# Attention and a routed two-layer expert network on one core: spacers that bring x and W1 to one residue modulo 512 bytes

## The chip, the core and the metric

The kernel runs on one core of a Trainium2 chip. The metric is device time in microseconds. Of the core's engines this text names PE (TensorE; its weight loads stand in a row of their own, PEld), DVE (VectorE), ACT (ScalarE), POOL (GpSimd) and SP (SyncE, here a DMA queue).

## What is computed

Shapes: 8 batches, 8 heads, 576 positions, head size 64; 8 experts, model width 512, hidden width 1024; all float32.

```python
kv = np.einsum('bhsd,bhse->bhde', k, v)
out = np.einsum('bhsd,bhde->bhse', q, kv)
rms = np.sqrt(np.mean(out * out, axis=-1, keepdims=True) + 1e-06)
x = (out / rms * g_norm)                      # transposed to (B, S, H * D)
...
logits = np.einsum('bsd,de->bse', x, w_gate)
local_gate = 1.0 / (1.0 + np.exp(-np.einsum('bsd,de->bse', x, w_local).squeeze(-1)))
for b in range(B):
    prev_e = -1
    for s in range(S):
        fresh_e = int(np.argmax(logits[b, s]))
        e = fresh_e if s == 0 or local_gate[b, s] < 0.5 else (prev_e if prev_e >= 0 else fresh_e)
        prev_e = e
        ...                                   # p: softmax of logits[b, s]
        h = np.maximum(x[b, s] @ w1[e], 0.0)
        out[b, s] = p[e] * (h @ w2[e])
```

Each of the 4608 tokens goes through the one expert that the routing names.

## The kernel before

**Up to about 167 us** the kernel computes the linear attention, writes its rows to DRAM, works out the routing, and does four 128-token blocks of expert 0: two together (`first_wide`, line 1079, from `xh`, `xl` that lie in an attention buffer) and two singly (`block`, line 1114, whose activations are the tiles `th`, `tl`).

**From there to the end** runs the loop of line 1442 over seven ranks, the other experts in order of their load. Each rank has 768 to 512 tokens, in two parts. The tokens' rows are gathered from DRAM (POOL), scaled, transposed and split (ACT, DVE) into a high and a low part: tiles `xh`, `xl` for the first part of a rank, `yh`, `yl` for the second, each of 4 depths by 384 columns (`xtiles(xp, HM, ...)`, lines 1412, 1459 and 1487). The matrices come by DMA into `wst` and are split into high and low parts in the same way (`wsplit`, line 257).

A float32-accurate product is made of three matmuls in the fp32r type, high by high, high by low, low by high (`split_mm`, line 1001; lines 1005, 1010, 1011). A part of a rank goes through

- a first product (`first_wide`): W1 is loaded as weights, 128 columns at a time, and x or y streams past it with 384, 352, 320 or 256 columns; 8 column blocks by 4 depths by 3 terms are 96 matmuls, accumulated in `ph`; ACT and DVE make `hh`, `hl` of it;
- a second product for each 128 tokens (`products`, line 1020): `hh`, `hl` as weights, W2 streams with 512 columns; 8 by 3 are 24 matmuls into `py` (a last block of 64 tokens goes through line 1055).

The order on PE, DVE, ACT and POOL is written by hand: it is the order of the code, with hooks (`then`, `hooks`, `tick`) that put scales, transposes, splits and gathers between the matmuls. Buffers come from stacked pools, so a tile's address is the sum of what lies before it. `pad` (line 157) puts a tile that nobody uses into a pool; its third argument counts 4-byte elements, 16 without it, and a pad of a name already seen is left out.

**Where the tiles lie.** The pool `xp` holds x, the six gather buffers `xr`, then y and the transposes' `xT`. Right behind it the pool `b` holds the W1 slots 4 to 7 and the W2 slots 4 and 5. The W1 slots 0 to 3 are in the pool `s`. `wsplit` gives a rank one group of four W1 slots and the next rank the other: rank 1 has slots 4 to 7, rank 2 has 0 to 3, and so on. The names in the trace leave the layer out: `w_4h` beside `ph` is slot 4 of W1, beside `py` slot 4 of W2. Inside all these tiles the steps between depths and column blocks are multiples of 512 bytes, so each operand of a matmul has the residue of its tile.

Of the kernel before, what the change touches and what calls it, by code (L numbers as in the profile page):

```python
# [22 lines left out]
def kernel(  # L23
# [124 lines left out]
    wpools = {}  # L148

    def wpool(nm, side="right"):  # L150
        wpools[nm] = wstack.enter_context(
            tc.tile_pool(name="w" + nm, bufs=1, side=side, reuse_waits="tile"))
        return wpools[nm]
# [3 lines left out]
    def pad(pool, nm, n=16):  # L157
        if nm not in padded:
            padded.add(nm)
            pool.tile([P, n], F32, name=nm)  # L160
# [85 lines left out]

    def wtile(pool, nm):
        if nm in ("w2_0h", "w2_4h"):
            pad(wpools[pool], "pad" + pool, 112 if pool == "s" else 48)
        t = wpools[pool].tile([P, 2 * DM], F32R, name=nm)  # L250
        if nm == "w2_0l":
            pad(wpools[pool], "past" + pool, 32)
        if nm == "w2_2l":
            pad(wpools[pool], "pad" + pool)
        return t

    def wsplit(e, i, two=False):
        t = staged.pop((e, i))

        if i < NW1:  # L260
            slot = (e * NW1 + i) % (2 * NW1)
            nm, pool = f"w1_{slot}", "s" if slot < NW1 else "b"
        else:
            slot = (e * NW2 + i - NW1) % (NW2 + 2)
            nm, pool = f"w2_{slot}", "scc"[slot] if slot < 3 else "d" if slot < NW2 else "b"
        hi, lo = (wtile(pool, nm + x) for x in "hl")
        low_ = split_w(hi, lo, t, i, e > 1)
        wt[e, i] = (hi, lo)

        def low(engine=nc.vector):  # L270
            i = low_(engine)
            if to_load:
                wload(*to_load.pop(0))
            return i

        if two:
            return low
        low()
# [800 lines left out]
    def first_wide(w, hh, hl, xh, xl, n=2 * P, then=(), each=None, late=0):  # L1079

        st = 2 if n <= 2 * P else 1
        then = list(then)

        def pairs(f, d0, d1):
            return [(w1s(w, d, f * P, P), (xh[:, d, 0:n], xl[:, d, 0:n])) for d in range(d0, d1)]

        if late:
            phs = [ps_h.tile([P, 1, n], F32, name="ph", tag="bank") for _ in range(late)]
            for f in range(late):
                split_mm(phs[f][:, 0], pairs(f, 0, ND - 1), last=False)  # L1090
                for what in then[f:f + 1]:
                    if what:
                        what()
            for f in range(late):
                split_mm(phs[f][:, 0], pairs(f, ND - 1, ND), first=False)
                relu_split(hh[:, f:f + 1, 0:n], hl[:, f:f + 1, 0:n], phs[f], n)
        for f in range(late, NF, st):
            ph = ps_h.tile([P, st, n], F32, name="ph", tag="bank")
            for x in range(st):
                split_mm(ph[:, x], pairs(f + x, 0, ND))  # L1100

            nl = n - n % P if n % P == D else n
            relu_split(hh[:, f:f + st, 0:n], hl[:, f:f + st, 0:nl], ph, nl)
            if nl < n:
                nc.vector.scalar_tensor_tensor(
                    hh[:, f:f + st, n:n + D], ph[:, :, nl:], 0.0,
                    hh[:, f:f + st, nl:n].bitcast(F32), op0=ALU.max, op1=ALU.subtract)
            if each:
                each()
            for what in then[f:f + st]:  # L1110
                if what:
                    what()
# [38 lines left out]
    def htiles(pool, n=2 * P):  # L1151
        return tuple(pool.tile([P, NF, n], F32R, name="h" + x) for x in "hl")

    def xtiles(pool, n, nm):
        return tuple(pool.tile([P, ND, n], F32R, name=nm + x, bufs=2 if nm == "t" else 1)
                     for x in "hl")
# [101 lines left out]
    xp = wpool("xp", "left")  # L1258
# [5 lines left out]
    def read(c, most):  # L1264
        return nc.values_load(cnt[0:1, c:c + 1], min_val=0, max_val=most)  # L1265
# [135 lines left out]
    def parts(r):  # L1401

        n = WIDTHS[r - 1]
        na = HM if n > 2 * HM - P else 2 * P
        bl = [Block(r, k, min(P, n - k * P), r == 1) for k in range(-(-n // P))]
        return bl[:na // P], bl[na // P:], na, n - na
# [2 lines left out]

    lots = {r: parts(r) for r in range(1, E)}  # L1410
    hs = htiles(z)
    xt = xtiles(xp, HM, "x")
    la, lb = lots[1][:2]
    for bl in la:
# [16 lines left out]
    def tick():  # L1431

        if todo:
            todo.pop(0)()

    def with_ticks(hooks):
        return sorted([*hooks, *((f, tick) for f in (2, 5))], key=lambda x: x[0])

    with tc.manual_schedule(engines=order):
        for bl in lb:  # L1440
            bl.gather()
        for r in range(1, E):
            la, lb, na, nb = lots[r]
            ma, mb_ = lots[r + 1][:2] if r + 1 < E else ([], [])
            todo = [what for bl in ma for what in bl.gathers()]
            own = [lambda j=j: wsplit(*j)
                   for j in ((r, NW1 + i) for i in range(NW2)) if j not in wt]
            nxt = [lambda i=i: wsplit(r + 1, i) for i in range(NW1 + NW2 // 2) if ma]
            hh, hl = htiles(z, HM)

            then = [None] * NF
            for x, what in enumerate(own):
                then[x if len(own) > 2 else 2 * x] = what
            for x, bl in enumerate(lb):
                then[NF - len(lb) + x] = bl.scale
            first_wide({i: wt[r, i] for i in range(NW1)}, hh, hl, *xt, n=na, then=then, each=tick)
            w = {i: wt[r, i] for i in range(NW1 + NW2)}
            pad(xp, "padx")
            yt = xtiles(xp, HM, "y")
            pad(xp, "pady")  # L1460
            turns = [lambda x=x, bl=bl: bl.turn(*yt, x * P) for x, bl in enumerate(lb)]
            for x, bl in enumerate(la):
                hooks = []
                for f in (1, 3, 5):
                    q_ = turns if f == 3 or f == 1 and x else nxt if x else []
                    if q_:
                        hooks.append((f, q_.pop(0)))
                bl.second(w, hh, hl, x * P, with_ticks(hooks))
            while todo:
                tick()  # L1470
            while turns:
                turns.pop(0)()
            hh, hl = htiles(z, HM)
            then = [None] * NF
            for x, bl in enumerate(ma):
                then[NF - len(ma) + x] = bl.scale
            if nxt:
                then[1] = nxt.pop(0)
            if nxt:
                then[3] = nxt.pop(0)  # L1480
            if not ma:

                nc.gpsimd.drain()  # L1483
                some = read(E, NT)
            todo = [what for bl in mb_ for what in bl.gathers()]
            first_wide(w, hh, hl, *yt, n=nb, then=then, each=tick)
            xt = xtiles(xp, HM, "x")
            turns = [lambda x=x, bl=bl: bl.turn(*xt, x * P) for x, bl in enumerate(ma)]
            for x, bl in enumerate(lb):
                left_ = len(lb) - x  # L1490
                hooks = []
                for f in (1, 3, 5, 6):
                    if turns and (f in (1, 5) and left_ > 1 or left_ == 1):
                        hooks.append((f, turns.pop(0)))
                    elif nxt and f == 3:
                        hooks.append((f, nxt.pop(0)))
                end = bl.second(w, hh, hl, x * P, with_ticks(hooks), not ma and left_ == 1)
            while todo:
                tick()
            assert not turns  # L1500
            while nxt:
                nxt.pop(0)()
# [33 lines left out]
```

## Time and profile before

| | us |
|---|---|
| three runs, median (lowest, highest) | 567.75 (565.28, 569.9) |
| the profiled execution, its own time | 562.02 |
| its span, first to last instruction | 560.2 |
| PE busy in the span | 544.4 |
| DVE, ACT, POOL busy | 302.5, 240.4, 231.2 |

The span holds what the engines did; 1.8 us of the execution's time lie around it. Matmuls overlap, so the sum of their durations is more than PE's busy time; what counts is when the next one starts. In a row of instructions the names are out<-in, with the buffer numbers left out.

### The profile page before, as it was taken

How to read it: one execution, taken by the hardware profiler on the slowest of the kernel's cores; microseconds unless marked ns; L12 is line 12 of the kernel's file. 1: busy time of each engine (PE TensorE's matmuls, PEld its weight loads, DVE VectorE, ACT ScalarE, POOL GpSimd, SP SyncE). 2: the span in 40 equal slices, each digit the busy share in tenths (PEclk: the TensorE clock that was granted, in tenths of full speed). 3: DMA queues.
4: the chain of work that ended last, by engine and by line, in shares of the span. 5: the costliest groups of instructions: out<-in, count | busy, mean ns of one | idle time of the engine just before them, and what ended most of it. 6: DMA issues, size and time to landing. Idle time of an engine off the chain costs nothing. (4 is left out here: it accounts for less than half of the span.)

```text
span 560.2 us, 11778 instructions
## 1 busy us (share of the span) xinstructions
PE 544.4 (97%) x4625; PEld 479.8 (86%) x4625; DVE 302.5 (54%) x633; ACT 240.4 (43%) x440; POOL 231.2 (41%) x299
## 2 busy tenths in 40 slices
PE   8999998999989999999999999999999999999996
PEld 5787876797769899898989898989799989989895
DVE  2127876699776436356464655465455636564510
ACT  2678775761354333334333334333334333534220
POOL 4344442323238435352553673347354535532001
PEclk9999999999999999999999999999999999999999
DMA  8999999673693353332533452335334433432000
GB/s 314 354 349 361 362 351 388 203 286 152 214 320 120 134 156 118 111 109 77 159 99 109 125 173 80 127 133 159 107 129 148 118 116 133 134 113 74 19 20 31
DMA packets 38302, 95.00 MB, mean 170 GB/s; under 512 B 6229, under 2 KB 6229, under 8 KB 38238
## 3 DMA queue, kind: packets, MB, share of 16 engines
q1 hardware_dynamic: 30448, 72.73, 37.1%
q0 software_dynamic: 7744, 21.41, 12.6%
q8 instruction: 38, 0.62, 0.5%
q14 instruction: 26, 0.21, 0.1%
q10 hardware_dynamic: 46, 0.02, 0.0%
HBM read 73.92 MB, written 20.88 MB: 169 GB/s over the span
## 5 line engine op out<-in xcount | busy, mean ns | idle before, releaser
L815 POOL DMA_INDIRECT xr<-xs,gid x120 | 132.7, 1106 | 36.6 <-issue 33.5
L1076 DVE SCALAR_TENSOR_TENSOR hl<-ph,hh 128x384 fp32r<-128x384 f32 (+3 forms) x94 | 52.3, 560 | 111.4 <-ACT hh L1075 108.6
L1041 POOL DMA_INDIRECT out_dram<-ot,sidr x34 | 35.1, 1032 | 170.9 <-ACT ot L1040 125.0
L1075 ACT ACTIVATE hh<-ph 128x384 fp32r<-128x384 f32 (+4 forms) x94 | 46.9, 502 | 118.9 <-PE ph L1011 118.9
L1040 ACT ACTIVATE ot<-py,pe 128x512 f32<-128x512 f32 (+1 forms) x36 | 24.7, 686 | 61.0 <-PE py L1011 29.0
L479 PE MATMUL po<-kvb,qT 128*64 128x146 f32 x512 | 40.4, 299 | 2.4 <-issue 2.4
L527 DVE TENSOR_REDUCE ms<-sq 128x9 f32<-128x576 f32 x32 | 22.6, 748 | 36.2 <-POOL sq L522 34.7
L479 PEld LDWEIGHTS po<-kvb,qT 128*64 128x64 f32 x512 | 31.2, 139 | 7.1 <-issue 5.7
L522 POOL TENSOR_TENSOR sq<-raw 128x576 f32<-128x576 f32 x13 | 16.8, 1290 | 37.2 <-ACT raw L492 22.3
L422 POOL COPY kvb<-kvp 64x128 f32<-64x128 f32 x64 | 18.9, 295 | 23.6 <-ACT kvp L408 19.3
L489 ACT COPY raw<-po 128x584 f32<-128x584 f32 x32 | 20.5, 640 | 16.9 <-PE po L485 14.2
L843 DVE TENSOR_TENSOR xr<-xr 128x512 f32<-128x512 f32 x38 | 26.2, 689 | 0.0
L404 PEld LDWEIGHTS po<-vt,kt 64*64 64x64 f32 x1152 | 20.1, 136 | 4.9 <-ACT raw L492 2.0
L836 ACT CAST yh<-xT 128x512 fp32r<-128x512 f32 x17 | 10.5, 620 | 29.9 <-DVE xT L832 29.9
L404 PE MATMUL po<-vt,kt 64*64 64x64 f32 x1152 | 22.7, 223 | 0.0
L832 DVE STREAM_TRANSPOSE xT<-xr 128x512 f32<-128x512 f32 x30 | 21.2, 706 | 0.4
L1005 PE MATMUL py<-w_1h,hh 128*128 128x512 f32 (+1 forms) x54 | 21.2, 393 | 0.0
L1005 PE MATMUL py<-w_0h,hh 128*128 128x512 f32 (+1 forms) x54 | 21.1, 391 | 0.0
L1011 PE MATMUL py<-w_0h,hl 128*128 128x512 f32 (+1 forms) x54 | 21.1, 391 | 0.0
L1010 PE MATMUL py<-w_0l,hh 128*128 128x512 f32 (+1 forms) x54 | 21.1, 390 | 0.0
L1011 PE MATMUL py<-w_1h,hl 128*128 128x512 f32 (+1 forms) x54 | 21.1, 390 | 0.0
L1010 PE MATMUL py<-w_1l,hh 128*128 128x512 f32 (+1 forms) x54 | 21.0, 389 | 0.0
(447 smaller groups left out, 1643.7 us busy)
## 6 DMA issues: line engine op xcount, KB each, us to landing
wst<-in_moe_w_dram SPq DMA_DIRECT2D x64, 512.0 KB, 3.8
xs<-raw SPq DMA_DIRECT2D x16, 584.0 KB, 6.0
kt<-in_k_dram SPq DMA_DIRECT2D x32, 288.0 KB, 5.0
vt<-in_v_dram SPq DMA_DIRECT2D x32, 288.0 KB, 5.1
qt<-in_q_dram SPq DMA_DIRECT2D x32, 288.0 KB, 5.1
xr<-xs,gid POOLq DMA_INDIRECT x120, 3.8
xs<-raw SPq DMA_DIRECT2D x4, 292.0 KB, 6.5
out_dram<-ot,sidr POOLq DMA_INDIRECT x36, 4.1
```

The lines of the kernel that those rows point to most:

```text
L404: nc.tensor.matmul(pk[half(b), x, 0:D], ks[b][half(x), cd], vs[b][half(x), cd], start=(c == 0), stop=(c == C - 1))
L479: nc.tensor.matmul(out[:, :, x * HW:(x + 1) * HW], qT[:, b, w, half(x)], kvb[:, o:o + PW], start=True, stop=True)
L527: nc.vector.tensor_reduce(mss[g][:, :, 2 * n + x], sqs.pop((s, x)), axis=AX.X, op=ALU.add)
L815: i = nc.gpsimd.indirect_dma_start(out=xr[:, u * PW:(u + 1) * PW], out_offset=None, in_=xs.rearrange("t (q w) -> (t q) w", w=PW), in_offse ...
L843: (engine or nc.vector).tensor_mul(xv, xv, r.unsqueeze(3).to_broadcast([P, NP, 2, D]))
L1005: mm = nc.tensor.matmul(ps, ah, bh, start=(first and i == 0), stop=False)
L1010: nc.tensor.matmul(ps, ah, bl, start=False, stop=False)
L1011: nc.tensor.matmul(ps, al, bh, start=False, stop=(last and i == n - 1))
L1040: nc.scalar.activation(ot[0:m], po[0:m], AF.Copy, scale=pe[0:m])
L1041: return nc.gpsimd.indirect_dma_start(out=outf, out_offset=bass.IndirectOffsetOnAxis(ap=idx[0:m], axis=0), in_=ot[0:m], in_offset=None, bo ...
L1075: nc.scalar.activation(hh, ps, AF.Relu)
L1076: nc.vector.scalar_tensor_tensor(hl, ps[:, :, 0:nl], 0.0, hh[:, :, 0:nl].bitcast(F32), op0=ALU.max, op1=ALU.subtract)
```

## The change

Spacers between buffers, and nothing else. A first spacer of 192 bytes is put ahead of x; the spacer ahead of y grows from 64 to 192 bytes; the spacer of 64 bytes behind y goes; the spacer ahead of slot 4 of W2 in the pool `b` grows from 192 to 448 bytes.

```diff
     def wtile(pool, nm):
         if nm in ("w2_0h", "w2_4h"):
-            pad(wpools[pool], "pad" + pool, 112 if pool == "s" else 48)
+            pad(wpools[pool], "pad" + pool, 112 if pool in "sb" else 48)
...
     hs = htiles(z)
+    pad(xp, "padw", 48)
     xt = xtiles(xp, HM, "x")
...
-            pad(xp, "padx")
+            pad(xp, "padx", 48)
             yt = xtiles(xp, HM, "y")
-            pad(xp, "pady")
```

The addresses in a partition that come out of it, and their residues modulo 512:

| tile | before | residue | after | residue |
|---|---|---|---|---|
| xh, xl of the ranks | 19168, 25312 | 224 | 19360, 25504 | 416 |
| yh, yl of the ranks | 46176, 52320 | 96 | 46496, 52640 | 416 |
| W1 slots 4 to 7 (first) | 60576 | 160 | 60832 | 416 |
| W1 slots 0 to 3 (first) | 171424 | 416 | 171424 | 416 |
| W2 slots 4, 5 (first) | 93536 | 352 | 94048 | 352 |
| W2 slots 0 to 3 | | 352 | | 352 |
| hh, hl | 118112, 130400 | 352 | 118112, 130400 | 352 |
| first gather buffer xr | 31456 | 224 | 31648 | 416 |
| xT | 58528 | 160 | 58784 | 416 |

The activations `th`, `tl` of expert 0's single blocks (residue 288) stay where they are. No instruction is moved on any engine. One wait differs in its count: the first cast into `xh` of the ranks on ACT (line 859) waits for DVE up to an earlier instruction, since `xh` no longer shares addresses with four small tiles of the routing.

## Rows read from the trace of the kernel before

**Rows 1.** The page: busy time by engine, and PE and its clock in 40 slices.

```profile
PE 544.4 (97%) x4625; PEld 479.8 (86%) x4625; DVE 302.5 (54%) x633; ACT 240.4 (43%) x440; POOL 231.2 (41%) x299
...
PEclk9999999999999999999999999999999999999999
```

**Rows 2.** Windows: busy time of each engine from 200 to 550 us.

```profile
core 0: us, PE busy (x) PEld busy (x) DVE busy (x) ACT busy (x) POOL busy (x), PEclk, DMA share, GB/s
200.00:550.00 350.00, 350.00 (x2015) 318.40 (x2014) 178.57 (x325) 127.55 (x191) 151.75 (x140) 1.00 0.35 112
```

**Rows 3.** PE groups by shape (count | busy us, mean ns | idle): 256 columns, two slots.

```profile
L1010 PE MATMUL ph<-xl,w_4h 128*128 128x256 f32 x24 | 6.7, 279 | 0.0
...
L1005 PE MATMUL ph<-xh,w_0h 128*128 128x256 f32 x16 | 4.5, 278 | 0.0
```

**Rows 4.** Timeline of PE: start, duration; 384 columns, and the second product between.

```profile
start us, us, engine line op out<-in xcount [idle before <-releaser]
202.39 0.34 PE L1005 MATMUL ph<-yh,w_4h 128*128 128x384 f32 x1
...
219.16 0.40 PE L1005 MATMUL py<-w_4h,hh 128*128 128x512 f32 x1
...
235.52 0.34 PE L1005 MATMUL ph<-xh,w_0h 128*128 128x384 f32 x1
...
252.16 0.40 PE L1005 MATMUL py<-w_2h,hh 128*128 128x512 f32 x1
```

**Rows 5.** Timeline of PE: first of 352 columns and first behind them, twice.

```profile
374.69 0.33 PE L1005 MATMUL ph<-yh,w_0h 128*128 128x352 f32 x1
...
390.06 0.39 PE L1005 MATMUL py<-w_4h,hh 128*128 128x512 f32 x1
...
428.28 0.33 PE L1005 MATMUL ph<-yh,w_4h 128*128 128x352 f32 x1
...
443.64 0.39 PE L1005 MATMUL py<-w_2h,hh 128*128 128x512 f32 x1
```

**Rows 6.** Timeline of PE: the same for 320 columns.

```profile
268.49 0.31 PE L1005 MATMUL ph<-yh,w_0h 128*128 128x320 f32 x1
...
282.56 0.39 PE L1005 MATMUL py<-w_2h,hh 128*128 128x512 f32 x1
```

**Rows 7.** Timeline of PE: the same for 256 columns, three of six stages.

```profile
297.10 0.28 PE L1005 MATMUL ph<-xh,w_4h 128*128 128x256 f32 x1
...
308.40 0.40 PE L1005 MATMUL py<-w_0h,hh 128*128 128x512 f32 x1
...
352.46 0.28 PE L1005 MATMUL ph<-xh,w_0h 128*128 128x256 f32 x1
...
363.76 0.40 PE L1005 MATMUL py<-w_4h,hh 128*128 128x512 f32 x1
...
406.51 0.28 PE L1005 MATMUL ph<-xh,w_4h 128*128 128x256 f32 x1
...
417.40 0.39 PE L1005 MATMUL py<-w_2h,hh 128*128 128x512 f32 x1
```

**Rows 8.** Timeline of PE: expert 0's single blocks, 14 and 18 first-product matmuls.

```profile
138.20 0.39 PE L1010 MATMUL ph<-w_0l,th 128*128 128x512 f32 x1
...
141.23 0.40 PE L1011 MATMUL ph<-w_0h,tl 128*128 128x512 f32 x1
...
150.11 0.40 PE L1005 MATMUL py<-w_3h,hh 128*128 128x512 f32 x1
...
151.50 0.39 PE L1005 MATMUL ph<-w_0h,th 128*128 128x512 f32 x1
...
155.45 0.40 PE L1011 MATMUL ph<-w_1h,tl 128*128 128x512 f32 x1
```

**Rows 9.** Timeline of ACT: the first cast into x of the ranks.

```profile
164.43 0.59 ACT L859 CAST xh<-pt 128x512 fp32r<-128x512 f32 x1 [1.93 <-PE pt L855]
```

**Rows 10.** Timeline of the weight loads: the one ahead of the matmul at 202.39.

```profile
202.17 0.19 PEld L1005 LDWEIGHTS ph<-yh,w_4h 128*128 128x128 f32 x1
```

## The prediction

> **What bounds the kernel now.** I read the page's engine totals first: PE is busy 544.4 us of a span of 560.2, and the clock row shows full speed (2.4 GHz, the higher of the two levels) in all 40 slices [rows 1]. Then the windows: from 200 to 550 us PE is busy for all of the 350 us, while DVE has 178.57, ACT 127.55, POOL 151.75 and the DMA engines a share of 0.35 [rows 2]. The reader is to see that no other engine and no transfer is waited for there. So the only thing that can move the time is the interval at which PE starts one matmul after the other. Busy time does not give that interval, because matmuls overlap: the grouped rows put a 256-column matmul at 278 or 279 ns, with eight as with any slot of W1 [rows 3], but they start every 0.11 to 0.12 us. I therefore took starts from the timeline: the first matmul of a stage, the first of the next, and the count that the code fixes between them (96 for a first product: 8 column blocks by 4 depths by 3 terms).
>
> The stages that the change touches are the fourteen first products of the ranks (x or y against W1): four with 384 columns, two with 352, two with 320, six with 256, 1344 matmuls in all. Their intervals, with the ideal of columns / 2.4 GHz taken off:
>
> - 384 columns, y on slots 4 to 7: (219.16 - 202.39) / 96 = 174.7 ns, 14.7 over 160.0. x on slots 0 to 3: (252.16 - 235.52) / 96 = 173.3, 13.3 over [rows 4].
> - 352 columns, y on slots 0 to 3: 15.37 / 96 = 160.1; y on slots 4 to 7: 15.36 / 96 = 160.0; both 13.4 over 146.7 [rows 5].
> - 320 columns: 14.07 / 96 = 146.6, 13.2 over 133.3 [rows 6].
> - 256 columns: x on slots 4 to 7, 11.30 / 96 = 117.7 and in a later rank, at the very same addresses, 10.89 / 96 = 113.4; x on slots 0 to 3, 11.30 / 96 = 117.7; that is 11.0 or 6.7 over 106.7 [rows 7]. Four of the six stages run at 117.7, two at 113.4.
>
> The second product is the kernel's own case of matched operands: hidden activations and W2 all lie at residue 352, in before as in after. Its interval at 512 columns is (235.52 - 219.16) / 72 = 227.2 ns [rows 4], 13.9 over 213.3.
>
> **The change part by part.** It adds and removes no instruction; PE, ACT and POOL have the same rows in the same order, and one buffer number differs on DVE and SP.
>
> *x and y beside W1.* Today the residues of W1 minus those of x or y are, modulo 512, 448 and 192 for x (slots 4 to 7, slots 0 to 3) and 64 and 320 for y. After, all are 0. No row shows a first product of a rank at 0, so its cost is bounded from both sides. The nearest rows are the second product's: matched, with the same kind of operands, the same weight loads, the same engine state. Matched costs 13.9 over the ideal there; unmatched costs 13.2 to 14.7 at 320 to 384 columns. The two slot groups give the same time within 0.1 ns at 352 and at 256 columns although their residues differ by 256 bytes, and one address pair gives both 113.4 and 117.7. So the overhead looks like one per matmul that addresses do not set, and I take: the matched first product pays what it pays today, with 384-column y stages (two of them) coming to the x stages' 173.3. That is 2 x 96 x 1.4 ns = 0.27 us less. The lower end of the sum, a gain, is the law that fits the cheapest rows: 113.4 / 106.7 = 1.063 and 227.2 / 213.3 = 1.065, against 1.08 to 1.10 in the other first products. If matched means 1.064 times the ideal at every width, then 384 columns go from about 174 to 170.2 (four stages, 3.8 ns), 352 from 160.1 to 156.1 (two, 4.0), 320 from 146.6 to 141.9 (two, 4.7), 256 from 117.7 to 113.5 (four, 4.2): 96 x (15.2 + 8.0 + 9.4 + 16.8) = 4.7 us less. The upper end, a loss, is that matched pays 13.9 at 256 columns too: 96 x (4 x 2.9 + 2 x 7.2) = 2.5 us more.
>
> One place speaks for the law. In the two single blocks of expert 0 the first product has 512 columns and its residues differ (activations at 288, W1 at 416): (141.23 - 138.20) / 13 = 233.1 ns and (155.45 - 151.50) / 17 = 232.4, some 5.5 ns over the matched 227.2 [rows 8]. But the matched second product just before, from 150.11 to 151.50, takes 1.39 / 6 = 231.7 [rows 8], so the place in the program explains most of that. This stage is not changed.
>
> *W1 slots 4 to 7, and W2 slots 4 and 5 behind them.* W1 moves by 256 bytes to the residue of slots 0 to 3; W2 moves by 512 and keeps 352. The writes into them (ACT, DVE) have other addresses and the same sizes. They run beside a PE that never waits from 200 to 550 us [rows 2]; cover gone, they would have to grow from 127.55 and 178.57 to near 350 us before they counted. Cost: nothing.
>
> *The x pool 192 bytes higher.* Its first tile no longer lies over four small routing tables, so the first cast into x on ACT waits for an earlier DVE instruction than it did. That cast had stood idle 1.93 us for PE's transposes, which come last [rows 9]; nothing queued behind it starts sooner. Cost: nothing. The gathered rows and the transposes' buffer move by whole multiples of 64 bytes.
>
> *The sum:* 562.02 us of the profiled execution less 0.3 gives 561.7. The profiled execution is 5.73 us under the median of the three runs, 567.75 (they spread from 565.28 to 569.9); the same difference on the median gives **567.5**.
>
> **The rivals.**
> 1. *Proportional law: matched reads save 4 to 5 ns at each width.* For it: the two ratios of 1.063 and 1.065, and the blocks' 233. Against it: 113.4 occurs with unmatched residues, and the same addresses also give 117.7. Price 4.7 us: 557.3 on the profiled execution, 563.0 on the median; 0.8%, just inside what counts as no change, so half of this case lies on each side once its own error is allowed for.
> 2. *The overhead in the first product is all conflict.* It would fall away: 96 x (4 x 14.0 + 2 x 13.4 + 2 x 13.2 + 4 x 11.0 + 2 x 6.7) = 16.0 us less, 546.0 and 551.8. A half-way version, down to the 6.7 of the cheapest stage, gives 96 x (4 x 7.3 + 2 x 6.7 + 2 x 6.5 + 4 x 4.3) = 7.0 us, 555.0 and 560.8. Against both: the matched second product still pays 13.9. The Trainium skill speaks for this rival: "TensorE: Matmul & The Clock Gate", section "Back-to-back issue gap", gives the gap of an isolated warm matmul as columns / 2.4 + 2.5 ns, by which the fourteen stages would give back 12.6 us. This trace does not reach that gap, matched or not: it would be 215.8 ns at 512 columns, and the second product takes 227.2.
> 3. *Slower: matched residues make the weight load and the streamed operand meet.* A weight load reads 128 columns, 512 bytes of a partition, and runs while the matmul before it streams (0.19 us from 202.17, while its own matmul starts at 202.39) [rows 4, 10]; if equal residues make them collide in the first product, each matmul could come to what the worst uninterrupted stretch has, 233 - 213.3 = 19.7 over, some 6 ns more: 1344 x 6 = 8.1 us, 570.1 and 575.8. It counts as slower from 5.7 / 1344 = 4.2 ns a matmul. Against it: the second product, equal residues, runs at 227.2.
> 4. *The change does nothing at all,* because PE reads both operands without regard to residue. The equal times of the two slot groups speak for it. Then 562.0 and 567.75, which can't be told from my forecast.
>
> **How the numbers follow.** No or next to no effect, my forecast with rival 4 and the 2.5 us of loss: 0.65. Rival 1: 0.20. Rival 2 with its half-way version: 0.09. Rival 3: 0.06. A measurement of this kernel tells about 1% (5.7 us) from no change. Faster by over 1%: all of rival 2 and about 0.08 of rival 1, 0.17. Slower: 0.05, as the lighter part of rival 3 stays under the bound. Within 1%: 0.78. The range takes in rival 1 (563.0), the half-way version (560.8), the upper bound of the sum (570.2) and some of the runs' spread, and leaves out the full rival 2 and rival 3: 560 to 571. The likeliest case alone: 565 to 570.
>
> **What would show it.** The starts of the first and last matmul of the same fourteen stages: my forecast wants about 173, 160, 147 and 113 to 118 ns; rival 1 wants 170, 156, 142 and 113.5; rival 2 at most 167; rival 3 near 180 at 384 columns. The second product should stay at 227, the blocks of expert 0 at 232 to 233, and PE should be busy for all of 200 to 545 us with no wait. I am wrong if the 352- and 320-column stages, which show one value each today, move by more than 2 ns, or if the span changes by over 3 us while the fourteen stages do not.

## The result: slower, by less than one per cent

The changed kernel takes 569.35 us (median of 21 runs, 565.08 to 575.42) against 565.13 us (21 runs, 560.42 to 571.18) for the kernel before: a ratio of 1.0081, 95% interval 1.0056 to 1.0106. Medians here and below are of all runs, while ratios leave out the slow ones, more than some 1.5% above the fastest of the same kernel, so a ratio is not always that of the two medians. The time lies inside the predicted range and within the 1% called "no change", but the forecast was 0.3 us faster and the kernel is slower by more than its interval. Five later sets of runs of the same program gave 1.0014 to 1.0069 (table below); the matmuls of the ranks explain 1.7 us of it, 1.003.

The profile taken with that result is of an execution of 575.42 us, in which PE waits in the ranks. Its page (busy time; PE's clock in 40 slices), and PE's waits from 190 us to the end (what waited, for what: us in total, times, longest):

```profile
PE 550.9 (96%) x4625; PEld 482.4 (84%) x4625; DVE 302.5 (53%) x633; ACT 239.2 (42%) x440; POOL 230.9 (40%) x299
...
PEclk9999999999999999999989999999999999999999
```

```profile
PE ph L1010 <- issue: 1.3, 2, 0.7
PE ph L1005 <- ACT yh L836: 1.3, 1, 1.3
PE ph L1005 <- issue: 0.9, 1, 0.9
PE ph L1010 <- DVE yl L837: 0.6, 2, 0.3
PE py L1010 <- issue: 0.6, 2, 0.3
```

Against [rows 2], where PE was busy for every microsecond of the ranks, these waits, 4.7 us in sum, are new. 1.9 us of them stand in first products of y whose last token block was cast late (`yh`, `yl`); for the other 2.8 us the profile shows no releaser ("issue"). PE lost more than the waits: from 288 to 290 us, behind a group of them, its granted clock is 0.51, the lower level (1.2 GHz), and 512-column matmuls start every 427 ns. In sum this profile takes 398.17 us from the first rank's first matmul to PE's last start. A second profile of the same program, of 560.50 us, has no such wait: PE is busy for all of the 345 us from 200 to 545. Its page and that window:

```profile
PE 544.4 (97%) x4625; PEld 480.1 (86%) x4625; DVE 302.3 (54%) x633; ACT 240.3 (43%) x440; POOL 237.5 (43%) x299
...
200.00:545.00 345.00, 345.00 (x1984) 314.45 (x1983) 178.09 (x324) 126.44 (x190) 156.87 (x140) 1.00 0.36 111
```

What residues do is read from this second profile, by the same starts as in [rows 4 to 7]:

```profile
164.12 0.44 PE L1005 MATMUL ph<-xh,w_4h 128*128 128x384 f32 x1
...
199.16 0.33 PE L1005 MATMUL ph<-yh,w_4h 128*128 128x384 f32 x1
...
215.80 0.39 PE L1005 MATMUL py<-w_4h,hh 128*128 128x512 f32 x1
...
265.11 0.30 PE L1005 MATMUL ph<-yh,w_0h 128*128 128x320 f32 x1
...
279.18 0.39 PE L1005 MATMUL py<-w_2h,hh 128*128 128x512 f32 x1
...
293.71 0.28 PE L1005 MATMUL ph<-xh,w_4h 128*128 128x256 f32 x1
...
305.22 0.40 PE L1005 MATMUL py<-w_0h,hh 128*128 128x512 f32 x1
...
371.52 0.32 PE L1005 MATMUL ph<-yh,w_0h 128*128 128x352 f32 x1
...
386.88 0.39 PE L1005 MATMUL py<-w_4h,hh 128*128 128x512 f32 x1
...
403.31 0.28 PE L1005 MATMUL ph<-xh,w_4h 128*128 128x256 f32 x1
...
414.83 0.40 PE L1005 MATMUL py<-w_2h,hh 128*128 128x512 f32 x1
...
553.17 0.39 PE L1011 MATMUL rbank<-w_1h,hl 128*128 128x512 f32 x1
```

| first product, columns | before, ns | after, ns | over columns / 2.4 after |
|---|---|---|---|
| 384, y (two stages) | 174.7 | 16.64 / 96 = 173.3 | 13.3 |
| 352 | 160.0, 160.1 | 15.36 / 96 = 160.0 | 13.3 |
| 320 | 146.6 | 14.07 / 96 = 146.6 | 13.3 |
| 256, four stages | 117.7 | 11.51 / 96 = 119.9 | 13.2 |
| 256, x of ranks 5 and 6 | 113.4 | 11.52 / 96 = 120.0 | 13.3 |

With equal residues the overhead is one number, 13.3 ns, at every width. That helps the two 384-column y stages (0.26 us), leaves 320 and 352 alone and costs all six 256-column stages: 4 x 0.20 + 2 x 0.63 = 2.1 us more, so 1.8 us more over the fourteen stages. From the first rank's first matmul to PE's last start the changed kernel takes 553.17 - 164.12 = 389.05 us; the kernel before, whose last start is at 554.69, takes 554.69 - 167.34 = 387.35, by its own timeline:

```profile
167.34 0.44 PE L1005 MATMUL ph<-xh,w_4h 128*128 128x384 f32 x1
...
554.69 0.39 PE L1011 MATMUL rbank<-w_1h,hl 128*128 128x512 f32 x1
```

The difference is **1.70 us**; the matmuls between the fourteen stages give back the 0.1. Two more profiles of the changed kernel (those of sets 3 and 4 of the table) have no wait in the ranks either and give 389.05 us each.

### The profile page after: what moved, and what is told of

It reads as the page before. It is cut to its first block, busy times and chain, and to the rows that moved or that the text cites. A ratio compares the mean times of both kernels' runs of the same rounds, so it can differ in the third digit from the quotient of the medians.

```text
span 573.6 us, 11778 instructions
## 1 busy us (share of the span) xinstructions
PE 550.9 (96%) x4625; PEld 482.4 (84%) x4625; DVE 302.5 (53%) x633; ACT 239.2 (42%) x440; POOL 230.9 (40%) x299
## 4 chain that ended last, share of the span: by engine, by line
PE 77%; DMA 7%; DVE 6%; issue 6%; ACT 3%; SPq 0%; POOLq 0%; DVEq 0%; ACTq 0%
PE ph L1010 11%; PE ph L1011 11%; PE ph L1005 11%; PE py L1010 9%; PE py L1005 9%; PE py L1011 9%; PE po L479 5%; DMA vt<-in_v_dram 4%; PE po L404 3%; PE pq L459 2%; PE py L1055 1%; PE po L485 1%; DMA qt<-in_q_dram 1%; DMA wst<-in_moe_w_dram 1%; PE pl L438 1%
## 5 line engine op out<-in xcount | busy, mean ns | idle before, releaser
L404 PE MATMUL po<-vt,kt 64*64 64x64 f32 x1152 | 24.2, 227 | 0.8 <-DMA vt<-in_v_dram 0.6
L836 ACT CAST xh<-xT 128x512 fp32r<-128x512 f32 x13 | 8.1, 622 | 32.0 <-DVE xT L832 32.0
```

Source lines behind the costliest of these rows:

```text
L404: nc.tensor.matmul(pk[half(b), x, 0:D], ks[b][half(x), cd], vs[b][half(x), cd], start=(c == 0), stop=(c == C - 1))
```

## The experiments

**What a second profile and more runs of the changed kernel show** (no edit).

> The changed kernel once more, for a second profile. Theory A (interval): all 256-column first products start every 119.9 ns instead of 117.7 or 113.4, and the 384-column y stages every 173.4 instead of 174.7; that is 96 x (4 x 2.2 + 2 x 6.5) - 2 x 96 x 1.3 = 1.8 us, and in an undisturbed profile PE has no wait in the ranks, so the time is 1.8 us over the kernel before. Theory B (late rows): PE waits in the ranks again, at the same places as in the first profile of the changed kernel (y of ranks 2, 4 and 6), 3 us or more in sum; the time is then 4 to 5 us over before.

Measured: 565.97 us against 564.40, ratio 1.0014 (0.9973 to 1.0055). All 256-column stages stand at 119.9, as in the rows above, and PE has no wait in the ranks. Theory B falls as a fixed part of the change.

**x and all that lies behind it moved by 512 bytes, no residue changed.**

```diff
+    pad(xp, "padw", 128)
     xt = xtiles(xp, HM, "x")
```

> The kernel before with 512 bytes put ahead of x: x, the gather buffers, y, xT and W1 slots 4 to 7 all move as far as in the change or further, but every residue modulo 512 is that of before. Theory A (interval, set by residues): the time of before within 0.3%, and the 256-column stages at 117.7 and 113.4 as before. Theory B (another address or the relaxed wait costs by itself): slower than before by 3 to 5 us, like the change.

Measured: 565.44 us, ratio 1.0015 (0.9978 to 1.0052); 256-column stages at 117.7 (four) and 113.4 (two), 384-column y at 174.7, all as before. The first of them, by its timeline:

```profile
293.35 0.28 PE L1005 MATMUL ph<-xh,w_4h 128*128 128x256 f32 x1
...
304.65 0.40 PE L1005 MATMUL py<-w_0h,hh 128*128 128x512 f32 x1
```

11.30 / 96 = 117.7. x starts at 19680 here, higher than in the change (19360), so it clears the four small tables too. So neither the higher addresses nor the relaxed wait on ACT set the intervals; the residues are what is left. The profile's stretch from the first rank to PE's last start, 389.10 us, can't be set beside the change's: it has breaks of its own, with 0.7 us of waits (a late cast into `yl`, a late `hl`).

**W1 slots 4 to 7 alone.**

```diff
-            pad(wpools[pool], "pad" + pool, 112 if pool == "s" else 48)
+            pad(wpools[pool], "pad" + pool, 112 if pool in "sb" else 48)
...
-            pad(xp, "pady")
+            pad(xp, "pady", 80)
```

> The kernel before with only W1 slots 4 to 7 brought to residue 416 (x stays at 224, y at 96). Theory A in the form that only equal residues of both operands cost: intervals as in before (117.7 or 113.4 at 256 columns, 174.7 or 173.3 at 384), the time within 0.3% of before. If W1's own place is what costs: some stages come to 119.9 and the time to 4 us over before.

Measured: 567.04 us, ratio 1.0029 (0.9985 to 1.0072), thirteen of the fourteen intervals those of before to 0.1 ns; the fourteenth, the 352-column y stage of rank 4, begins with a wait of 0.2 us for a late cast into `yl` and then settles at 159.9. A move of W1 by 256 bytes changes nothing, which is what a period of 256 would do too.

**A map of residues behind the last rank.** It was built on the changed kernel; the offset o runs over 0, 4, 1, 5, 2, 6, 3, 7.

```diff
+        for n, order_ in ((2 * P, (0, 4, 1, 5, 2, 6, 3, 7)), (HM, (0, 4, 1, 5, 2, 6, 3, 7)),
+                          (DM, (0, 4, 1, 5, 2, 6, 3, 7)), (2 * P, (7, 3, 6, 2, 5, 1, 4, 0))):
+            for o in order_:
+                for f in range(4):
+                    ph = ps_h.tile([P, 1, n], F32, name="pm", tag="bank")
+                    split_mm(ph[:, 0], [(w1s(w, d, f * P + 16 * o, P), w1s(w, (d + 1) % ND, 0, n))
+                                        for d in range(ND)])
```

> The changed kernel with a map behind its last rank: weights from W1 at column offsets of 0 to 7 times 64 bytes, W1's next depth streamed past them with 256, 384 and 512 columns, 48 matmuls each, so residues that differ by 0, 64, ... 448 bytes. Theory A: at difference 0 the interval is the ideal plus 13.3 ns at each width (120.0, 173.3, 226.6); at other differences it is lower at 256 columns (113 to 118) and up to 6 ns higher at 512 columns (232 to 233, as in expert 0's single blocks). If residues don't matter: one value at each width, whatever the difference. The program is some 270 us longer by the map.

The timeline of PE, first matmul of a group of 48 each: 256 columns at offsets 0, 256 and 64 bytes and what follows; 512 columns likewise; then offset 320 bytes at 256 columns on the way back.

```profile
558.26 0.28 PE L1005 MATMUL pm<-w_5h,w_4h 128*128 128x256 f32 x1
...
564.01 0.28 PE L1005 MATMUL pm<-w_5h,w_4h 128*128 128x256 f32 x1
...
569.76 0.28 PE L1005 MATMUL pm<-w_5h,w_4h 128*128 128x256 f32 x1
...
575.42 0.28 PE L1005 MATMUL pm<-w_5h,w_4h 128*128 128x256 f32 x1
...
670.92 0.40 PE L1005 MATMUL pm<-w_5h,w_4h 128*128 128x512 f32 x1
...
681.84 0.39 PE L1005 MATMUL pm<-w_5h,w_4h 128*128 128x512 f32 x1
...
692.72 0.40 PE L1005 MATMUL pm<-w_5h,w_4h 128*128 128x512 f32 x1
...
703.92 0.40 PE L1005 MATMUL pm<-w_5h,w_4h 128*128 128x512 f32 x1
...
782.10 0.28 PE L1005 MATMUL pm<-w_5h,w_4h 128*128 128x256 f32 x1
...
787.56 0.28 PE L1005 MATMUL pm<-w_5h,w_4h 128*128 128x256 f32 x1
```

The intervals by weights' residue minus streamed operand's, from starts like these:

| difference, bytes | 256 columns, first pass | way back | 384 | 512 |
|---|---|---|---|---|
| 0, 256 | 119.8, 120.0 | 120.0, 120.0 | 173.5, 173.4 | 227.4, 226.7 |
| 64, 320 | 117.8, 117.8 | 113.3, 113.7 | 176.7, 176.7 | 233.4, 233.4 |
| 128, 384 | 118.7, 118.7 | 118.6, 118.7 | 175.9, 175.9 | 232.4, 232.4 |
| 192, 448 | 117.8, 117.8 | 117.8, 117.8 | 173.3, 173.3 | 228.9, 228.9 |

Three things follow. Differences that are 256 apart give the same interval in each pass: the period is 256 bytes, not 512. Equal residues are best at 512 columns (6 ns) and worst at 256. And 64 gives 117.8 on the one pass and 113.3 to 113.7 on the other, so what went before counts too.

**x alone at 416, with y and slots 4 to 7 at their old residues**: the test of the period in the kernel itself.

```diff
+    pad(xp, "padw", 48)
     xt = xtiles(xp, HM, "x")
...
-            pad(xp, "padx")
+            pad(xp, "padx", 96)
```

> Only x goes to residue 416; y stays at 96 and W1 slots 4 to 7 at 160 (all behind x moves by 512 bytes). Weights minus x is then 0 in the ranks on slots 0 to 3 (2, 4, 6) and 256 in the ranks on slots 4 to 7 (1, 3, 5, 7). If the period is 512 bytes, only ranks 4 and 6 have their 256-column x stage at 119.9 ns, and 3, 5, 7 stay at 117.8 or 113.4. If the period is 256 bytes, as the map has it, all five stand at 119.9. y stays at 174.7 (384 columns) and 117.8 (256) in both.

Measured (timeline: x of rank 3, on slots 4 to 7; x of rank 4, on slots 0 to 3; y of rank 7):

```profile
297.97 0.28 PE L1005 MATMUL ph<-xh,w_4h 128*128 128x256 f32 x1
...
309.48 0.40 PE L1005 MATMUL py<-w_0h,hh 128*128 128x512 f32 x1
...
357.49 0.28 PE L1005 MATMUL ph<-xh,w_0h 128*128 128x256 f32 x1
...
369.00 0.40 PE L1005 MATMUL py<-w_4h,hh 128*128 128x512 f32 x1
...
545.68 0.28 PE L1005 MATMUL ph<-yh,w_4h 128*128 128x256 f32 x1
...
556.99 0.40 PE L1005 MATMUL py<-w_4h,hh 128*128 128x512 f32 x1
```

11.51 / 96 = 119.9 in rank 3 at a difference of 256 as in rank 4 at 0, and likewise in 5, 6 and 7; y stays at 11.31 / 96 = 117.8. The period is 256 bytes. The 384-column y stage of rank 3, behind a wait of 1.3 us and ten matmuls at the lower clock (starts 320 ns apart), settled at 176.7 in place of 174.7: the first map's value at the same difference. This execution (575.0 us, one run) shows the same late casts of y as the first profile of the change, and more of them:

```profile
PE ph L1005 <- ACT yh L836: 3.8, 3, 1.3
PE py L1005 <- ACT hh L1075: 1.0, 1, 1.0
PE ph L1010 <- DVE yl L837: 0.9, 3, 0.3
```

**The map in steps of 16 bytes** (the same edit with `4 * o`, 16 offsets, three column blocks).

> The map behind the changed kernel once more, with steps of 16 bytes over 256 (36 matmuls at each of 256, 384 and 512 columns). If what counts is the distance of the two operands within 256 bytes, the interval changes in steps or ramps with it, between the values of the first map: at 512 columns 226.7 at 0, 233.5 at 64, 232.4 at 128, 228.9 at 192; at 384 columns 173.4, 176.7, 175.9, 173.4; at 256 columns 120.0 at 0, 117.8, 118.7, 117.8 or 113.4. If only whole steps of 64 bytes count, the values between two of them repeat the lower one. The program is some 240 us longer by the map.

| difference, bytes | 512 columns | 384 columns |
|---|---|---|
| 0 | 227.9 | 173.7 |
| 16, 32, 48, 64 | 233.3, 233.1, 233.3, 233.4 | 173.5, 173.4, 173.6, 173.3 |
| 80, 96, 112, 128 | 232.0, 234.2, 233.2, 232.4 | 173.3, 173.3, 173.3, 176.0 |
| 144, 160, 176, 192 | 233.4, 233.1, 230.0, 229.2 | 177.3, 176.7, 173.5, 173.3 |
| 208, 224, 240 | 232.0, 233.1, 226.7 | 175.7, 176.6, 176.5 |

Steps of 16 bytes count: at 512 columns 16 bytes already cost 5 to 6 ns, and only 0 and 240 are cheap. There is no ramp. At 384 columns 64 now gives 173.3 where the first map had 176.7, a second sign of several rhythms at one difference; in the ranks of before the same difference gives 174.7. Each value comes from one pass in one order. At 256 columns the values lie between 116.7 and 120.1, with no clear order.

**The differences that the map recommends**: 192 in all fourteen stages, 0 in expert 0's single blocks.

```diff
-            pad(wpools[pool], "pad" + pool, 112 if pool == "s" else 48)
+            pad(wpools[pool], "pad" + pool, 112 if pool in "sb" else 48)
...
-    pad(z, "padh", 40)
+    pad(z, "padh", 72)
...
-        pad(z, "padz", 128)
+        pad(z, "padz", 96)
...
-            pad(xp, "padx")
+            pad(xp, "padx", 48)
...
-            pad(xp, "pady")
+            pad(xp, "pady", 48)
```

> From the kernel before: y goes to residue 224 like x, so that weights minus streamed operand is 192 modulo 256 in all fourteen first products, and the activations of expert 0's single blocks go to 416, so that theirs is 0 in place of 128. By the map (period of 256 bytes; the best difference depends on the width) the 384-column y stages come from 174.7 to 173.4 ns, the 320- and 352-column stages stay within 0.2 ns of 146.6 and 160.0, the 256-column stages stay at 117.8 or 113.4, and the 48 first-product matmuls of the single blocks go from 232 to 233 ns to 226 to 227 ns. In sum 0.3 + 0.3 us less than before: a ratio of 0.999, which the time alone cannot tell from 1. If residues don't act by these differences, the blocks stay at 232 to 233.

Measured: 564.96 us against 567.65, ratio 0.9981 (0.9923 to 1.0038). A second set of runs:

> The kernel with differences of 192 (and 0 in expert 0's single blocks) for more timed runs: 0.5 us less than before by its stages, so a ratio of 0.999; against the changed kernel of the same call it should be 2.3 us (0.4%) less.

560.78 us against 561.25, ratio 0.9988 (0.9967 to 1.0010). Its timeline, a 384-column y stage and stretches of the two single blocks:

```profile
202.41 0.34 PE L1005 MATMUL ph<-yh,w_4h 128*128 128x384 f32 x1
...
219.06 0.40 PE L1005 MATMUL py<-w_4h,hh 128*128 128x512 f32 x1
...
140.46 0.39 PE L1010 MATMUL ph<-w_3l,th 128*128 128x512 f32 x1
...
141.37 0.39 PE L1011 MATMUL ph<-w_0h,tl 128*128 128x512 f32 x1
...
153.98 0.39 PE L1010 MATMUL ph<-w_3l,th 128*128 128x512 f32 x1
...
155.56 0.39 PE L1011 MATMUL ph<-w_1h,tl 128*128 128x512 f32 x1
```

The y stage is at 16.65 / 96 = 173.4. In the blocks the first nine or ten matmuls (behind a break of the stream, or behind the change from a second product) still take 224 to 237 ns, apart from one of 323 right behind the break; then the stream settles: 0.91 / 4 = 227 and 1.58 / 7 = 226. In before it never settled there [rows 8]. So the blocks' 232 to 233 was a matter of residues, but only the settled part of the 48 matmuls is won: 0.1 us in the two stretches of [rows 8], where 0.3 were expected for the blocks. The other stages are as expected, and the stretch from the first rank to PE's last start is 387.02 us, 0.33 less than before. The time cannot tell that from nothing.

**What sets the cheap rhythm of 113.4.** On the kernel of the last experiment, extra matmuls with 96 weight columns stand ahead of a 256-column first product.

```diff
+        for _ in range(kick):
+            pk = ps_h.tile([P, 1, n], F32, name="pk", tag="bank")
+            nc.tensor.matmul(pk[0:96, 0], w[0][0][:, 0:96], xh[:, 0, 0:n], start=True, stop=True)
```

> From the kernel with differences of 192 in all fourteen first products: ahead of four 256-column first products stand 1 (rank 3, x), 2 (rank 4, x), 3 (rank 7, x) and 6 (rank 7, y) extra matmuls whose weights have 96 columns, results unused. The two stages that run at 113.4 (x of ranks 5 and 6) follow a last token block of 96 tokens, whose second product loads weights of 96 columns; the four at 117.8 follow blocks of 64 or 128 tokens. If a short weight load puts the stream into the cheaper rhythm, the stages behind it run at 113.4 too, from some number of extra matmuls on. If the rhythm comes from something else, they stay at 117.8.

One extra matmul (rank 3) left its stage at 117.8, two (rank 4) brought it to 113.4, three and six (rank 7) left theirs at 117.8; the time was 560.68 us (one run). Number or place? Two everywhere, at unequal and at equal residues:

> From the kernel with differences of 192 everywhere: two extra matmuls with 96 weight columns (results unused, some 0.12 us each) ahead of all four 256-column first products that run at 117.8. If two short loads set the rhythm, all six 256-column stages stand at 113.4 and the time from the first rank's first matmul to PE's last is 4 x 0.42 less and 8 x 0.12 more than without them, 0.7 us less (386.7 us). If it was the place in rank 4 and not the number, only rank 4 changes and the stretch gets 0.5 us longer.

> The changed kernel (equal residues) with the same two extra matmuls ahead of the same four stages. If equal residues hold the stream in one rhythm whatever comes before it, as ranks 5 and 6 of the changed kernel suggest, all six stages stay at 119.9 and the stretch is 1 us longer than 389.4. If the rhythm can be set here too, the four stages come to 113.4.

The timeline of the first (rank 3: the extra pair, the stage, the next), then of the second:

```profile
293.59 0.28 PE L1085 MATMUL pk<-xh,w_4h 128*96 128x256 f32 x1
...
293.82 0.28 PE L1005 MATMUL ph<-xh,w_4h 128*128 128x256 f32 x1
...
304.71 0.39 PE L1005 MATMUL py<-w_0h,hh 128*128 128x512 f32 x1
```

```profile
300.42 0.28 PE L1005 MATMUL ph<-xh,w_4h 128*128 128x256 f32 x1
...
311.94 0.40 PE L1005 MATMUL py<-w_0h,hh 128*128 128x512 f32 x1
```

With unequal residues all six stages now run at 10.89 / 96 = 113.4; with equal ones all stay at 11.52 / 96 = 120.0. At each of the places where one, three or six did nothing, two do it: the number counts. Equal residues hold the stream in one rhythm with and without the pair. The PSUM buffers, which the extra matmuls take from the same seven in turn, don't explain it: ahead of x in rank 7 both kernels have taken six extra ones, and one runs at 117.8, the other at 113.4. Why two do it and one, three and six do not stays open, and as no run had extra matmuls with 128 weight columns, whether the 96 matter is not shown. The kernel with two extra matmuls took 563.66 us (557.98 to 570.98) against 565.53, ratio 0.9963 (0.9916 to 1.0010): ahead of both kernels by its 256-column stages, not by its time. In its profile the stretch is 387.28 us, where 386.7 were expected: the four stages are 1.7 us shorter, the four pairs cost 0.24 us each, and breaks in three second products, which are not in the profile of the 192 kernel's second set, cost 1.2 us. The one with equal residues took 568.25 us (one run).

**More runs of the changed kernel.** Set 2 has its runs of the kernel before in common with the first set of the 192 kernel, sets 3 and 4 with the second, set 5 with the last experiment:

> The changed kernel a third time, for its time: the stages account for 1.8 us (0.3%). If that is all that the change costs, the ratio to the kernel before is 1.001 to 1.006; if there is a second cost that the profiles do not show, 1.007 to 1.010 as in the first measurement.

> The changed kernel for more timed runs. Ratios so far: 1.0081, 1.0014 and 1.0069 to the kernel before. If the first products are the whole cost (1.8 us of 565), ratio 1.003; if there is a second cost of like size that no profile shows, 1.006 to 1.008.

> The same kernel again in the same call, so that the spread between two sets of runs of one program is seen. Equal programs: the two ratios differ by chance alone, and the stages of its profile are those of the other profiles of the changed kernel to 0.1 ns.

> The changed kernel for one more set of timed runs, with kick2 in the same call. By its stages 1.7 us over the kernel before: a ratio of 1.003. A ratio of 1.007 or more would speak for a second cost.

| set | changed, us | before, us | ratio (95% interval) |
|---|---|---|---|
| result | 569.35 | 565.13 | 1.0081 (1.0056 to 1.0106) |
| 1 (after_again) | 565.97 | 564.40 | 1.0014 (0.9973 to 1.0055) |
| 2 (after_third) | 571.07 | 567.65 | 1.0069 (1.0011 to 1.0127) |
| 3 (after_fourth) | 562.47 | 561.25 | 1.0016 (0.9994 to 1.0039) |
| 4 (after_fifth) | 562.40 | 561.25 | 1.0021 (1.0001 to 1.0040) |
| 5 (after_sixth) | 568.65 | 565.53 | 1.0030 (0.9984 to 1.0077) |

The five later sets all have the stages' 1.003 in their intervals; the first has not. Sets 3 and 4, with the narrowest intervals, give 1.2 us. What the first set had beyond 1.7 us is not settled. Late casts of y, as in its profile, are in the profile of set 5 too (rank stretch of 395.34 us); that of set 2 (390.87 us) has waits without a shown releaser. Such breaks are also in the profiles of kernels whose residues are the old ones (the 512-byte shift) or only partly changed, so no profile ties them to the change. Nor is the part ahead of the ranks steady: in the first set's profile the first rank starts at 169.75 us, in the second's at 164.12, in that of before at 167.34.

## Why the prediction missed the direction

- *The step that failed* is the value taken for x and y beside W1: "the matched first product pays what it pays today". It was bounded correctly: the upper end of the sum, "matched pays 13.9 at 256 columns too", priced at 2.5 us, is what happened (13.3 instead of 13.9, 2.1 us). What the timed result holds beyond that stays open. Choosing zero inside -4.7 to +2.5 was wrong. The nearest row, the matched second product, said 13.9, and the 256-column stages stood below that at 11.0 and 6.7; the choice should have gone by the row for all widths.
- *The reason given for zero was a misreading.* The two slot groups' equal times were taken as a sign that addresses do not matter, since their residues differ by 256 bytes. With a period of 256, which the map and the x-only kernel show, they are the same residue. In before, W1 minus x was 192 and W1 minus y 64 on both slot groups, modulo 256. Rival 4 rested on the same misreading and falls.
- *The blocks of expert 0* (233.1 and 232.4 ns) were put down to their place in the program, because a matched stretch of six just ahead ran at 231.7. The difference there is 128, for which the map gives 232.4, and the six were still settling.
- *Rival 1* was right that the blocks' 233 against 227.2 is an effect of residues at 512 columns, and wrong that it is a proportion: matched costs a constant 13.3 ns, so narrow stages lose. *Rival 2* falls with it. *Rival 3* had the sign and not the mechanism: no collision of 6 ns a matmul, 1.3 ns on average (1.7 us over 1344).
- *Right:* 384-column y stages from 174.7 to 173.3 (0.26 us); 320 and 352 columns unmoved; the second product still at 227; no cost from the moved W1, W2 and gather buffers or the relaxed wait (by the intervals of the 512-byte shift and the W1-only kernel); PE busy without a wait through the ranks, in the undisturbed profile.

## What to carry to other kernels

When PE never waits, take the interval between starts stage by stage, with the ideal taken off, and set it beside the residues of the two operands; test a suspected period with operands that differ by half of it before reading "no difference" as "no effect". Bring weights and streamed operand to one residue for wide matmuls (512 columns here), and not for narrow ones (256). A few nanoseconds a matmul come out of a profile exactly, where the timed runs could tell 1.7 us from nothing only in part of the sets.

## What the runs showed of the hardware

- The interval of this stream, which loads weights for each matmul, depends on the two SBUF addresses, in steps of at most 16 bytes: 226.7 to 234.2 ns at 512 columns, 173.3 to 177.3 at 384, 113.3 to 120.1 at 256, all at the full clock of 2.4 GHz. The first map and the x-only kernel show a period of 256 bytes. That it is their difference and not each address shows where kernel and map have one difference at other residues: 0 gives 227 ns at 512 columns in both, 128 gives 232 to 233, and 192 gives 117.8 ns at 256 and 173.3 to 173.4 at 384.
- Equal residues give columns / 2.4 + 13.3 ns at the five widths measured (256, 320, 352, 384, 512 columns). The Trainium skill, "TensorE: Matmul & The Clock Gate", section "Step-by-step: what each phase is for", says that loading the next tile's weights does not steal SBUF read bandwidth from the running matmul, since PE has two independent read ports. The runs show that the two reads are not without effect on the stream: the same instructions start up to 6 ns further apart with other addresses (512 columns). Which part of PE or SBUF does it, no run shows.
- At unequal residues one and the same stream has more than one steady rhythm (117.8 and 113.4 ns at 256 columns, held for all 96 matmuls), and what runs ahead picks it: two extra matmuls with 96 weight columns did. The stages behind a token block of 96 tokens run at 113.4 as well; that such a block is the cause is not shown.
